# Turning the expert outputs by transposing transfers in place of TensorE turns, batches 0 to 6

## The chip, the cores and the metric

The kernel runs on one core of a Trainium2 chip. The time is device microseconds of one execution; lower is better. Three runs of the kernel before took 242.09 to 243.47 us, with a median of 242.59 us. A trace is one further execution, taken by the hardware profiler. Its engines are PE (TensorE: matmuls and turns; its weight loads are listed as PEld), ACT (ScalarE), DVE (VectorE), POOL (GpSimd) and SP (SyncE, which here only issues DMAs).

## What is computed

Two stages over 8 batches of 576 tokens. The first is attention with 8 heads of 64 and a window of 32 tokens to either side. Its output, 576x512 per batch, goes through four attention experts: each projects it to q, k and v of width 64, does causal attention, and projects back to 512 with its own `wo`. A gate picks two of the four experts for each token and weights them.

```
scores = scale * np.matmul(q, k.transpose(0, 1, 3, 2))        # window of 32
x = (softmax(scores) @ v).transpose(0, 2, 1, 3).reshape(B, S, 512)
logits = x @ w_gate                                           # top 2 of 4, softmax over them
for e in range(4):
    qe, ke, ve = x @ wq[e], x @ wk[e], x @ wv[e]
    a = causal_softmax(scale * (qe @ ke.transpose(0, 2, 1)))
    out += weight_of_e * (a @ ve @ wo[e])
```

## The kernel before

The whole program is one list of steps, `ORDER`, written out by hand. Each engine gets its instructions in the order in which the steps stand in the list, and works them off in that order; the framework adds the semaphores from what each step reads and writes. A step is a name with digits, then `@` with its banks of PSUM, and `:` with the engine that does it: `a` ACT, `v` DVE, `g` POOL. `ot31:v@0` is thus step `ot` for batch 3 and expert pair 1, on DVE, from bank 0. All eight banks are one tile `PS`, dealt out by the numbers in the list.

Loads (`lq`, `lk`, `lv`: q, k and v), the moves on chip that pair heads (`mv`, four DMAs each, L366) and the stores (`st`, L727 and L730) are all issued by SP. A load also waits until PE has reached the load's place in the list (`load`, L195 to L200), so that SP can't run ahead of it; `mv` and `st` wait only for their data. SP issues in the order of the list too: a DMA whose data isn't ready holds up those behind it.

For one batch the steps that matter here run as follows. The four experts are worked in two pairs `j`.

- `po` (L640, PE): attention weights times values, into two banks.
- `oe` (L649, DVE): divides by the row sums, multiplies by the gate, and writes `OE`, 128 tokens x (5 token tiles x 2 experts x 64) in bf16. There are two such buffers, one a pair.
- `pt` (L658, PE): turns `OE` by five matmuls against the identity, 128x128 each, into one bank.
- `ot` (L663, ACT or DVE): copies that bank into `OTT`, expert width on the partitions and tokens along the row. `OTT` has two buffers, one for even and one for odd batches, and a half in each for a pair.
- `py` (L703, PE): times `wo`, both pairs added in PSUM; three parts, of 256, 256 and 64 tokens.
- `ye` (L719, ACT or DVE) copies the result out of PSUM and `st` stores it.

Batch 7 is the last, and its second pair is worked in three parts (`pw`, `ow`, `tw`, `uw`), so that the end of the program overlaps better. Its first pair uses `po`, `oe`, `pt` and `ot`.

The helpers `mm` (L189) and `turn_pe` (L192) issue all matmuls and all turns, so the profile shows those at L190 and L193; copies by `copy` stand at L182 (ACT) and L184 (DVE, POOL). Several stages share L190: the names of the tiles tell them apart. `PS<-WO,OTT` is `py`, `PS<-ident_bf,OE` is `pt` (and `tw`), `PS<-T` is the window scores (`sc`), `PS<-WV,XTB` is `pv`.

Of the kernel before, what the change touches and what calls it, by code (L numbers as in the profile page):

```python
# [20 lines left out]
HS = 288  # L21
# [3 lines left out]
NOE = 2  # L25
# [24 lines left out]
    po01@2 pt00@0 oe01@2 ot00:a@0 vc20:g qc31:g pp111@4 kc31:g mv31 pe111:a@4 lv32 lv33 ps102@6 mk2100:g vc21:g  # L50
    pt01@0 se100 ps103@1 xe103@1 xe102@6 se102 tq400:e qc40:g ps110@4 xe110@4 se110 pv11@3 ve11:a@3 av23@1 av20@6
    ot01:v@0 un23@1 mk3011:g py02@5 ye02:a@5 av24@0 lq410:e ps113@1 xe113@1 lk410:e un20@6 tk400:e ps112@4 xe112@4
    un24@0 ps111@6 xe111@6 py01@2 av21@4 un21@4 av22@6 un22@6 ye01:a@2 se113 sc311@02 ex3111@2 sc310@46 tq410:e
    ex3110@0 kc40:g mv40 st02 mk3001:g ex3101@6 se112 ex3100@4 lk500:e mk3010:g xt20@2 xf20:a@2 xt21@0 xf21:a@0
    xt22@6 lv30 xf22:v@6 se101 se103 po10@4 oe10@4 py00@2 ye00:a@2 sc400@06 ex4000@0 st01 ex4001@6 lq500:e
    mk3101:g lv42 sc401@24 xb20:g ex4011@4 se111 po11@0 lv34 lk510:e qc41:g ex4010@2 pt10@7 xb22:v xb21:g tk410:e
    pp201@5 pe201:a@5 pp200@2 kc41:a lv41 ga2@6 pe200:a@2 ps200@2 tk500:e ps203@4 st00 xe203@4 mv41 oe11@0 ps202@0
    xe202@0 xe200@2 ot10:v@7 pt11@7 ot11:a@7 gt2 pp210@4 mk3100:v mk3000:g vc31:g pe210:v@4 tq500:e pp211@0
    mk3110:g mk3111:g av33@2 pv21@7 un33@2 vc30:g av31@4 un31@4 lq510:e mk4010:g qc50:g ve21:a@7 pe211:a@0 ge2
    lv43 av34@7 un34@7 py11@0 ye11:a@0 mk4001:g py10@2 ye10:a@2 py12@7 ye12:a@7 av30@4 gm2 gu2@6 av32@0 xt32@6  # L60
    un30@4 xf32:a@6 sc410@24 un32@0 kc50:g mv50 xb32:g lv52 mk4011:v ex4101@4 mk4101:g ex4100@2 mk4100:g sc411@06
    ex4110@0 tq510:e qc51:g mk4110:g lk600:e lv40 xt31@4 xf31:a@4 lq600:e se200 xb31:v xt30@2 xf30:a@2 pv20@0
    ve20:v@0 ps213@2 ex4111@6 mk4111:g lv44 vc41:g xe213@2 se213 xb30:v tk510:e vc40:g ps212@4 xe212@4 mk4000:g
    sc501@26 ex5010@2 ex5011@6 sc500@04 ex5000@0 lv53 mk5000:g tk600:e ex5001@4 pp300@2 pp301@0 pe300:a@2 kc51:a
    se203 ps201@4 xe201@4 tq600:e pe301:a@0 ps211@2 ga3@7 xe211@2 gt3 kc60:g mv51 gm3 pp311@5 pe311:a@5 ps210@0
    xe210@0 se210 lv51 ps302@2 xe302@2 se211 pv31@4 av42@5 un42@5 ge3 ve31:a@4 vc50:g av43@0 un43@0 av40@2 un40@2
    ps301@5 xe301@5 lk610:e se301 av44@4 un44@4 qc60:a pp310@0 pe310:a@0 gu3@7 xt41@4 xf41:v@4 mk5010:g ps300@2
    xe300@2 se202 av41@6 un41@6 ps303@0 sc511@24 xe303@0 mv60 se212 mk5001:v ex5110@2 ex5111@4 lq610:e sc510@06
    lv54 lv50 mk5110:g tk610:e kc61:v lq700:e ex5101@6 ex5100@0 xt40@2 xf40:a@2 xb41:g xb40:g pv30@4 ve30:a@4
    xt42@0 xf42:v@0 sc600@26 ex6001@6 xb42:g ex6000@2 lk710:e mk5101:v sc601@04 ex6011@4 ex6010@0 lk700:e pp400@6  # L70
    se201 po20@2 mk5011:g pe400:a@6 tq610:e qc61:g ps313@0 xe313@0 ps312@4 oe20@2 tq700:e ps311@6 xe311@6 pp411@0
    pt20@2 lq710:e xe312@4 ot20:a@2 pe411:a@0 mk5100:g po21@6 oe21@6 pp401@4 vc51:g ga4@3 mk5111:g pe401:a@4
    ps403@6 xe403@6 ps401@4 xe401@4 ps310@0 xe310@0 tk700:e kc70:g mk6001:g pv41@2 ve41:a@2 av51@6 un51@6 qc70:g
    gt4 ge4 av52@4 un52@4 av50@0 se310 pt21@2 ot21:a@2 se302 st11 un50@0 mv61 pv40@6 mv70 gm4 ve40:a@6 xt50@4
    gu4@3 mk6011:g ps402@0 av54@2 un54@2 lv60 xf50:a@4 xb50:g lv64 se401 av53@6 lv70 un53@6 xe402@0 sc610@24
    ex6100@2 lv62 ex6101@4 lv63 sc611@06 ps400@2 ex6111@6 xe400@2 tq710:e mk6101:g py21@4 pp410@6 pe410:v@6
    ex6110@0 ye21:a@4 lv61 st10 lv71 se402 xt51@2 xt52@0 xf52:v@0 xf51:a@2 se312 xb52:a mk6100:g sc701@46 ex7010@4
    sc700@02 ex7001@2 xb51:v pp500@4 ex7000@0 mk6000:g tk710:e lv73 pp501@2 st12 ex7011@6 se303 se313 se311 po31@6
    oe31@6 lv72 pe501:a@2 pp511@2 pe511:v@2 st21 mk6111:g se300 po30@0 oe30@0 pe500:a@4 qc71:a ps503@6 ps502@4
    xe503@6 mk6010:v xe502@4 ps411@2 xe411@2 vc60:g ga5@7 gt5 ps410@0 xe410@0 ps501@5 ge5 pt31@4 ot31:v@4 pp510@2  # L80
    pt30@4 pe510:v@2 mk6110:g kc71:g vc61:g py20@0 xe501@5 gm5 av61@2 av60@5 ot30:a@4 un61@2 ye20:a@0 gu5@7 un60@5
    av63@0 un63@0 av62@2 un62@2 py22@7 ye22:v@7 ps413@4 xe413@4 av64@6 mv71 sc711@04 un64@6 ex7110@0 xt60@2
    ex7111@4 se502 xt62@6 st22 lv74 xf62:v@6 xf60:a@2 xb60:v py31@0 mk7011:g sc710@46 ye31:a@0 st31 ex7101@6 se413
    mk7110:g ex7100@4 mk7100:v xt61@2 xf61:a@2 ps412@0 xe412@0 mk7111:g pv50@6 se501 st20 se403 se400 po40@2
    oe40@2 ga6@0 ve50:a@6 gt6 ps513@6 xe513@6 mk7001:g ps500@4 xb62:g ps510@2 xe500@4 pt40@1 xb61:g xe510@2 vc71:v
    pp601@6 pe601:a@6 mk7000:g pp600@4 pe600:a@4 ge6 se410 ot40:v@1 se411 se412 po41@2 pp611@4 pe611:a@4 py30@6
    mk7010:g se500 ye30:a@6 pv61@1 py32@4 ye32:a@4 ve61:a@1 oe41@2 gm6 gu6@0 vc70:g av72@2 un72@2 ps602@6 xe602@6
    ps600@4 av73@0 mk7101:g un73@0 av70@2 un70@2 xe600@4 ps603@6 ps601@4 xe603@6 pt41@0 ot41:v@0 xe601@4 pp610@6
    pe610:a@6 ps511@4 ps512@2 xe512@2 se601 se512 xe511@4 se510 st30 se503 av74@0 un74@0 av71@6 pv51@0 un71@6
    py42@1 ve51:a@0 st32 ye42:v@1 st42 xt72@2 xf72:a@2 xt71@4 xf71:a@4 xb72:g xt70@6 xf70:a@6 xb70:v xb71:v  # L90
    ps611@0 py41@2 py40@4 ye41:a@2 ye40:a@4 po50@6 xe611@0 pv60@2 ve60:a@2 pp700@0 se600 st41 oe50@6 ps610@6
    xe610@6 pe700:v@0 se602 ps612@2 xe612@2 se513 st40 se511 po51@4 pp710@0 oe51@4 pt50@2 pp711@6 se611 se612
    ot50:v@2 pe711:a@6 pt51@2 pe710:v@0 ot51:a@2 se603 po60@4 ps613@6 se610 xe613@6 se613 ps711@0 ps710@2 xe710@2
    se710 xe711@0 pp701@6 pe701:a@6 oe60@4 pt60@4 po61@2 oe61@2 py50@0 ye50:a@0 st50 ot60:a@4 py51@6 ye51:v@6
    ps702@2 py52@5 ye52:a@5 st51 pv71@0 ga7@1 ve71:v@0 gt7 xe702@2 se702 st52 ps701@6 ps703@2 xe703@2 ps700@4
    se703 xe701@6 se701 xe700@4 pt61@0 ot61:v@0 pv70@2 gm7 py60@6 ge7 ye60:a@6 ve70:v@2 py61@4 st60 ye61:a@4
    ps712@2 st61 xe712@2 se711 gu7@1 pw710@0 ow710@0 se700 po70@6 oe70@6 py62@4 ye62:a@4 st62 ps713@0 tw710@5
    se712 pt70@6 ot70:v@6 pw711@7 ow711@7 uw710:a@5 py70@4 tw711@7 uw711:v@7 xe713@0 se713 pw712@6 ye70:a@4 st70
    py71@0 ye71:a@0 st71 ow712@6 tw712@7 uw712:a@7 py72@7 ye72:v@7 st72
# [4 lines left out]
def kernel(  # L104
# [84 lines left out]
    def mm(*a, **kw):  # L189
        last_pe[0] = nc.tensor.matmul(*a, **kw)  # L190
# [363 lines left out]

    def pp(c, b, j, n, b0):
        W = XTB[b % 2]
        for half in range(2):
            for dt in range(NDT):
                mm(PS[:, b0 + half, 0:HS], WQK[j][n][:, dt, :], W[:, dt, HS * half:HS * half + HS],
                   start=(dt == 0), stop=(dt == NDT - 1))  # L560
# [5 lines left out]
    def pv(c, b, part, b0):  # L566
        W = XTB[b % 2]
        if part == 0:
            for t in range(4):
                for dt in range(NDT):  # L570
                    mm(PS[:, b0 + t // 2, 256 * (t % 2):256 * (t % 2) + 256], W[:, dt, 128 * t:128 * t + 128], WV[:, dt, :],
                       start=(dt == 0), stop=(dt == NDT - 1))
        else:
            for dt in range(NDT):
                for j in range(2):
                    mm(PS[64 * j:64 * j + 64, b0, 0:128], W[:, dt, 512:576], WV[:, dt, 128 * j:128 * j + 128],
                       start=(dt == 0), stop=(dt == NDT - 1), skip_group_check=True)
# [14 lines left out]
    def ps(c, b, j, ch, b0):  # L592
        Q = QKE[(2 * b + j) % len(QKE)]
        for kt, lo, hi, at in CHUNKS[ch]:
            for eo in range(2):
                r = slice(64 * eo, 64 * eo + 64)
                if ch < 3:
                    mm(PS[:, b0 + eo, at:at + hi - lo], Q[r, 1, 128 * kt:128 * kt + 128], Q[r, 0, lo:hi],
                       start=True, stop=True, skip_group_check=True)
                else:  # L600

                    mm(PS[:, b0 + eo, 0:64], Q[r, 1, 512 - 64 * j:640 - 64 * j], Q[r, 0, 512:576],
                       start=True, stop=True, skip_group_check=True)
# [61 lines left out]


# [107 lines left out]
```

## Time and profile before

| | |
|---|---|
| median of three runs | 242.59 us (242.09 to 243.47) |
| the profiled execution | 243.22 us; span of its instructions 240.3 us |
| granted TensorE clock | 0.997 |
| busy: PE, DVE, ACT, POOL | 213.4, 190.9, 164.8, 144.8 us |
| DMA packets of SP's queue | 56864, 46.94 MB, 70.5% of 16 engines' span |
| turns of `OE` by PE | 80 matmuls, 7.5 us |
| copies into `OTT`, ACT and DVE | 9 and 9 |

Times in the profile are us from the first instruction, durations in ns where they are so called. A group of instructions is given by line, engine, operation, the tiles out<-in, the shapes, then count, busy us and mean ns, and the idle time just before them with what ended it. "SPq" marks DMA instructions of SP. The span is divided among stages that overlap: while one batch is in the experts, the next ones are in the window attention and in loading.

### The profile page before, as it was taken

What the parts mean: (1) busy time and instruction counts of PE and PEld (TensorE: products, weight loads), DVE (VectorE), ACT (ScalarE), POOL (GpSimd) and SP (SyncE); (2) the same over time, 40 slices, a digit from 0 to 9 for tenths busy, and PEclk for the clock granted to TensorE, in tenths of its full rate; (3) what the DMA queues carried; (4) which work ended last, traced back from release to release, by engine and by line L of the source; (5) the groups of instructions that cost most, each with busy time, mean ns of one, the idle gap of its engine ahead of it and who ended that gap; (6) DMA issues with size and microseconds to landing.
All of it is one profiled execution on the core that took longest, in us unless ns stands there. A gap on an engine that the chain in (4) does not pass through costs nothing.

```text
span 240.3 us, 10580 instructions
## 1 busy us (share of the span) xinstructions
PE 213.4 (89%) x4537; PEld 166.5 (69%) x4548; DVE 190.9 (79%) x350; ACT 164.8 (69%) x260; POOL 144.8 (60%) x189
## 2 busy tenths in 40 slices
PE   7877789797998999789999999989899959999981
PEld 2656676676876778569777888867597738776650
DVE  4789998697797969998999899678876995554770
ACT  2665467886689577556895886686829748967761
POOL 7005162444897796955998997699709961621310
PEclk9999999999999999999999999999999999999998
DMA  6999898999799889987976887698605120130555
GB/s 211 303 268 296 195 292 213 283 303 240 243 257 267 228 237 290 285 244 169 274 157 185 226 286 255 154 208 222 194 5 176 45 100 14 58 144 3 199 196 196
DMA packets 57486, 48.79 MB, mean 203 GB/s; under 512 B 40544, under 2 KB 43104, under 8 KB 57440
## 3 DMA queue, kind: packets, MB, share of 16 engines
q1 hardware_dynamic: 56864, 46.94, 70.5%
q10 hardware_dynamic: 576, 1.18, 1.4%
q8 instruction: 35, 0.57, 1.0%
q14 instruction: 11, 0.09, 0.1%
HBM read 30.42 MB, written 9.44 MB: 166 GB/s over the span
## 4 chain that ended last, share of the span: by engine, by line
PE 57%; DVE 15%; POOL 7%; issue 7%; DMA 5%; ACT 4%; SPq 2%; ACTq 0%; DVEq 0%; POOLq 0%
PE PS L190 50%; PE PS L193 6%; POOL A L422 4%; DVE T L184 3%; DMA V<-in_v_dram 3%; DVE T L317 2%; DMA T<-T 2%; ACT XTF L182 2%; SPq L196 2%; ACT A L418 2%; PE PS L237 1%; POOL V L184 1%; DVE OE L655 1%; POOL ATE L619 1%; DVE XN L451 1%
## 5 line engine op out<-in xcount | busy, mean ns | idle before, releaser
L422 POOL TENSOR_TENSOR A<-A,MASKP 128x576 f32<-128x576 f32 x40 | 57.6, 1448 | 5.0 <-ACT A L418 4.8
L619 POOL TENSOR_SCALAR_AFFINE_SELECT ATE<-ATE 128x256 bf16<-128x256 bf16 (+1 forms) x80 | 32.0, 419 | 38.6 <-ACT ATE L614 30.7
L614 ACT ACTIVATE ATE<-PS 128x1024 bf16<-128x1024 f32 x48 | 47.5, 1029 | 6.4 <-PE PS L190 6.4
L418 ACT ACTIVATE A<-PS 128x576 f32<-128x576 f32 x64 | 38.2, 652 | 14.0 <-PE PS L190 13.4
L190 PE MATMUL PS<-V,A 128*64 128x65 f32 (+1 forms) x1280 | 39.7, 223 | 4.8 <-POOL V L184 1.8
L190 PEld LDWEIGHTS PS<-V,A 128*64 128x64 f32 (+1 forms) x1280 | 36.1, 132 | 9.3 <-issue 3.0
L190 PE MATMUL PS<-T 64*64 64x128 f32 (+3 forms) x1280 | 39.7, 263 | 1.2 <-ACT XTF L182 0.6
L190 PEld LDWEIGHTS PS<-T 64*64 64x64 f32 x1280 | 33.7, 133 | 4.5 <-issue 1.8
L184 POOL COPY V<-V 64x1536 f32<-64x1536 f32 (+1 forms) x14 | 24.1, 1723 | 18.7 <-DMA V<-in_v_dram 16.5
L317 DVE STREAM_TRANSPOSE T<-qn 128x1152 f32<-128x1152 f32 x14 | 32.6, 2329 | 3.2 <-PE PS L190 2.7
L317 DVE STREAM_TRANSPOSE T<-kn 128x1152 f32<-128x1152 f32 x14 | 32.3, 2330 | 0.8 <-PE PS L190 0.5
L182 ACT COPY XTF<-PS 128x1024 f32<-128x1024 f32 (+1 forms) x21 | 17.2, 832 | 10.1 <-PE PS L193 8.3
L184 POOL CAST XTB<-XTF 128x128 bf16<-128x128 f32 (+1 forms) x21 | 15.5, 758 | 13.3 <-ACT XTF L182 12.9
L182 ACT COPY Y<-PS 128x1024 f32<-128x1024 f32 (+1 forms) x20 | 16.8, 858 | 9.4 <-PE PS L190 6.4
L451 DVE TENSOR_TENSOR XN<-PS,RC 128x512 f32<-128x512 f32 x32 | 22.1, 691 | 1.3 <-DVE RC L450 0.2
L190 PE MATMUL PS<-WO,OTT 128*128 128x512 bf16 (+1 forms) x85 | 18.6, 341 | 2.4 <-ACT OTT L182 1.1
L190 PE MATMUL PS<-WV,XTB 128*128 128x256 bf16 (+1 forms) x192 | 18.5, 256 | 2.0 <-DVE OTT L184 1.9
L182 ACT CAST QKE<-PS 128x576 bf16<-128x576 f32 x25 | 15.9, 642 | 5.4 <-PE PS L190 5.2
L190 PE MATMUL PS<-QKE 64*128 64x64 bf16 (+4 forms) x192 | 17.5, 277 | 2.0 <-DVE OE L655 1.4
L190 PE MATMUL PS<-XTB,WK 128*128 128x288 bf16 x128 | 18.3, 286 | 0.0
L190 PE MATMUL PS<-XTB,WQ 128*128 128x288 bf16 x128 | 18.0, 286 | 0.0
L190 PEld LDWEIGHTS <-XTB 128*128 128x128 bf16 (+1 forms) x192 | 14.3, 102 | 5.0 <-issue 3.4
(88 smaller groups left out, 319.0 us busy)
## 6 DMA issues: line engine op xcount, KB each, us to landing
V<-in_v_dram SPq DMA_DIRECT2D x32, 256.0 KB, 5.3
out_dram<-Y SPq DMA_DIRECT2D x16, 512.0 KB, 3.3
kn<-in_k_dram SPq DMA_DIRECT2D x28, 288.0 KB, 4.9
qn<-in_q_dram SPq DMA_DIRECT2D x28, 288.0 KB, 4.8
T<-T SPq DMA_DIRECT2D x56, 144.0 KB, 3.8
V<-in_v_dram SPq DMA_DIRECT2D x8, 128.0 KB, 5.6
out_dram<-Y SPq DMA_DIRECT2D x16, 64.0 KB, 3.1
qn<-in_q_dram SPq DMA_DIRECT2D x2, 320.0 KB, 4.8
```

Of the source, the lines that this page charges most:

```text
L182: nc.scalar.copy(o, i)
L184: eng(c).tensor_copy(o, i)
L190: last_pe[0] = nc.tensor.matmul(*a, **kw)
L193: last_pe[0] = nc.tensor.transpose(*a)
L196: r = q_.dma_start(o, i)
L237: nc.tensor.matmul(one(a[-1]), WARM[:, 0:128], WARM, start=True, stop=True, skip_group_check=True)
L317: nc.vector.transpose(T.rearrange("q h (p o) -> q h o p", o=18)[:, :, o0:o1, :], x[:, :, o0:o1, :])
L418: nc.scalar.activation(AT[(2 * b + g) % NAT_][half][p], two(b0)[:, :, 0:HS], EXP, scale=scale_att)
L422: eng(c).tensor_tensor(out=ap, in0=ap, in1=MASK[:, None, HS * half:HS * half + HS].to_broadcast([128, 2, HS]), op=MULT)
L451: nc.vector.tensor_tensor(out=XN[T // 2][:, T % 2, :].rearrange("p (t h d) -> p h t d", t=4, h=8), in0=u[:, :, 0:64].rearrange("p h (d t) ...
L614: nc.scalar.activation(chunk(A, ch), two(b0), EXP, scale=scale_moe)
L619: nc.gpsimd.affine_select(ap, ap, pattern=[[0, n], [1, w]], compare_op=IS_GE, fill=0.0, base=0, channel_multiplier=-1)
```

## The change

For batches 0 to 6, each `pt` and its `ot` are replaced by one step `dt`: a transposing DMA from `OE` to `OTT`, issued by SP, 14 in all. It stands in the list where `pt` stood, and the `ot` is gone. Batch 7 stays as it was. All other steps, their order, their banks and engines are the same. The transfer writes all 640 columns of its half of `OTT`, the copy wrote 576; nothing reads the last 64.

```diff
+    def dt(c, b, j):
+
+        nc.sync.dma_start_transpose(OTT[b % 2][:, j, :].rearrange("p (t c) -> p t c", c=128),
+                                    OE[(2 * b + j) % NOE][:, :, :, :].rearrange("p t e d -> p (t e d)"))
...
-    po01@2 pt00@0 oe01@2 ot00:a@0 vc20:g qc31:g pp111@4 kc31:g mv31 pe111:a@4 lv32 lv33 ps102@6 mk2100:g vc21:g
-    pt01@0 se100 ps103@1 xe103@1 xe102@6 se102 tq400:e qc40:g ps110@4 xe110@4 se110 pv11@3 ve11:a@3 av23@1 av20@6
-    ot01:v@0 un23@1 mk3011:g py02@5 ye02:a@5 av24@0 lq410:e ps113@1 xe113@1 lk410:e un20@6 tk400:e ps112@4 xe112@4
+    po01@2 dt00 oe01@2 vc20:g qc31:g pp111@4 kc31:g mv31 pe111:a@4 lv32 lv33 ps102@6 mk2100:g vc21:g dt01 se100
+    ps103@1 xe103@1 xe102@6 se102 tq400:e qc40:g ps110@4 xe110@4 se110 pv11@3 ve11:a@3 av23@1 av20@6 un23@1
+    mk3011:g py02@5 ye02:a@5 av24@0 lq410:e ps113@1 xe113@1 lk410:e un20@6 tk400:e ps112@4 xe112@4 un24@0 ps111@6
...
-    se703 xe701@6 se701 xe700@4 pt61@0 ot61:v@0 pv70@2 gm7 py60@6 ge7 ye60:a@6 ve70:v@2 py61@4 st60 ye61:a@4
+    se703 xe701@6 se701 xe700@4 dt61 pv70@2 gm7 py60@6 ge7 ye60:a@6 ve70:v@2 py61@4 st60 ye61:a@4 ps712@2 st61
```

The DMAs on SP's queue around the new steps, in their order, are then: `lk400 dt00 mv31 lv32 lv33 dt01 lq410`; `lk510 dt10 lv41 st00 mv41 dt11 lq510`; `lk700 dt20 lq710 dt21 st11 mv61 mv70`; `st21 dt31 dt30 mv71`; `st20 dt40 dt41 st30`; `st40 dt50 dt51 dt60 st50 st51 st52 dt61 st60`.

The diff also gives the matmul steps `pp`, `pv`, `ps` and `py` a way to write only half of the partitions at a time, for steps marked `q`. No step of the list is marked so, and these matmuls are the same as before.

## The prediction

> **What bounds the kernel now.** The page first. Its share of the chain of work that ended last says who sets the end:
>
> ```profile
> PE 57%; DVE 15%; POOL 7%; issue 7%; DMA 5%; ACT 4%; SPq 2%; ACTq 0%; DVEq 0%; POOLq 0%
> ```
>
> TensorE (PE) is on the chain more than half the time, so taking work off PE can pay, but only where PE is what everything waits for. Hence the second view, the chain in order of time. Its columns are start in us, us, and what:
>
> ```profile
> 68.05 7.02 DMA V<-in_v_dram
> 75.19 1.90 POOL V L184
> 77.14 3.89 PE PS L190 x107
> 81.08 4.93 PE PS L190 x127
> ...
> 99.28 0.41 PE PS L193 x5
> ...
> 171.61 0.46 DVE OTT L184
> 172.11 0.44 PE PS L193 x5
> ...
> 224.33 0.39 PE PS L193 x5
> ```
>
> The reader is to see two things. Up to 77.14 the chain runs through a load of V, so the two turns of batch 0 (`pt00`, `pt01`, at 73 and 75 us) are not on it. The pieces "L193 x5" are the turns of the expert outputs that are on it: nine of them, the first and the last shown, 3.31 us together; and one copy out of PSUM, 0.46 us.
>
> **What goes.** The groups of instructions, with count, busy us and mean ns:
>
> ```profile
> L193 PE MATMUL PS<-ident_bf,OE 128*128 128x128 bf16 x80 | 7.5, 220 | 1.7 <-DVE OTT L184 0.9 <-DVE OE L655 0.8
> ...
> L182 ACT COPY OTT<-PS 128x576 bf16<-128x576 bf16 x7 | 4.5, 642 | 0.3 <-PE PS L193 0.3
> ...
> L184 DVE COPY OTT<-PS 128x576 bf16<-128x576 bf16 x8 | 3.6, 451 | 1.1 <-PE PS L193 1.1
> ```
>
> Seventy of the 80 turns go, 70/80 x 7.5 = 6.6 us of PE, with seven ACT copies (7 x 0.642 = 4.5 us) and seven DVE copies (7 x 0.451 = 3.2 us). The copies lie beside PE work except the one on the chain. So the gain is bounded by 0 and by 6.6 us of PE plus 0.46 us plus one more wait, which the PE timeline shows in brackets:
>
> ```profile
> 195.42 0.41 PE L190 MATMUL PS<-WV,XTB 128*64 128x128 bf16 x8 [1.85 <-DVE OTT L184]
> ```
>
> There `pv61` waits 1.85 us for the copy `ot40`; but PE then waits again, for POOL, so the chain passes it by. Upper bound 6.6 + 0.46 + 1.85 = 8.9 us. I take what the chain holds: 3.31 + 0.46 = **3.8 us gained**. What is late next there is PE itself, on the following step of the list.
>
> **What comes.** Fourteen transfers on SP's queue, each 128x640 bf16 = 160 KB, from `OE` to `OTT`. The trace has no transposing transfer, so its two costs are bounded by neighbours: how long SP is held, and how long from issue to landing. First the on-chip moves of `mv` (ns min/median/max of the issue, and us to landing), then from the page a load, `mv` again with its size, and a small store, then the landing of all loads of L196:
>
> ```profile
> L366 SPq DMA_DIRECT2D T<-T x56: 508/588/1592, 25.3 to 171.0; - x56
> ...
> DMA to landing us min/median/max: 2.4/3.8/5.6
> ```
>
> ```profile
> V<-in_v_dram SPq DMA_DIRECT2D x32, 256.0 KB, 5.3
> ...
> T<-T SPq DMA_DIRECT2D x56, 144.0 KB, 3.8
> ...
> out_dram<-Y SPq DMA_DIRECT2D x16, 64.0 KB, 3.1
> ```
>
> ```profile
> DMA to landing us min/median/max: 2.8/5.2/9.0
> ```
>
> Held: 0.51 to 1.59 us, I take `mv`'s median, 0.59. Landing: 2.4 to 9.0 us. By place and size `mv` is nearest (3.8); by piece it is the load of V, which moves rows of 64 f32 = 256 bytes, as the transfer moves 128 bf16 = 256 bytes of a token tile (5.3). I take **4.5 us**, between them, while loads run, and 3.1 (the small store's) in the last 30 us, where SP issues stores alone.
>
> The Trainium skill speaks against the change: "VectorE: DVE Perf Modes", section "The three transpose paths", gives 1309 ns for a 128x128 bf16 block by DMA and 390 by TensorE. Here a TensorE turn takes 220 ns, so the second figure isn't this kernel's; no run yet shows the first. Five blocks one after the other would make 6.5 us of landing, an estimate from that page, and the sum below would then come out near 260 us.
>
> **Where it falls on the path.** SP works its queue in order. A transfer waits there for its `oe`, and behind it wait the loads, moves and stores of the list; its reader is `py`, on PE, which is in order too. The distance from the turn to `py` was a matter of the list, which stays. Three places are too short.
>
> *Batch 0.* On SP the order is `dt00 mv31 lv32 lv33 dt01`. SP's timeline (`mv31`, then the two loads of V), the expert output that `dt01` needs, and the PE step that reads it (`py02`):
>
> ```profile
> 74.07 2.46 SPq L366 DMA_DIRECT2D T<-T  x4
> 76.64 2.68 SPq L196 DMA_DIRECT2D V<-in_v_dram  x2
> ```
>
> ```profile
> 73.85 0.82 DVE L655 TENSOR_TENSOR OE<-PS,RG 128x640 bf16<-128x640 f32 x1
> ```
>
> ```profile
> 78.94 0.27 PE L190 MATMUL PS<-WO,OTT 128*64 128x256 bf16 x1
> ```
>
> The output is there at 74.67, but SP is through `lv33` only at 76.64 + 2.68 = 79.32, plus 0.59 for `dt00` = 79.91. Landing at 79.91 + 4.5 = 84.4. `py02` wanted it at 78.94 (the V chain sets that time, the turns saved don't). PE stands **5.5 us**.
>
> *Batch 1.* `dt11` comes right behind `mv41`, in a stretch where SP issues back to back:
>
> ```profile
> 99.33 2.86 SPq L366 DMA_DIRECT2D T<-T  x4
> ```
>
> ```profile
> 104.43 1.04 PE L190 MATMUL PS<-WO,OTT 128*128 128x512 bf16 x3
> ```
>
> `mv41` ends at 102.19, `dt10` ahead of it adds 0.59, landing at 102.78 + 4.5 = 107.28. `py11` without the turn `pt11` comes at 104.43 - 0.41 = 104.02: **3.3 us**.
>
> *Batch 6.* `dt61` stands behind the stores of batch 5 (`st52` last), and `py60` follows one step of PE later:
>
> ```profile
> 223.45 1.98 SPq L730 DMA_DIRECT2D out_dram<-Y  x2
> ```
>
> ```profile
> 226.30 1.03 PE L190 MATMUL PS<-WO,OTT 128*128 128x512 bf16 x3
> ```
>
> Issue at 225.43, landing at 225.43 + 3.1 = 228.53; `py60` is due at 226.30 - 0.39 = 225.91: **2.6 us**.
>
> The other eleven I cost at nothing, since their `py` is far off. The tightest is `dt51` (its `oe51`, then `py50`):
>
> ```profile
> 213.92 0.82 DVE L655 TENSOR_TENSOR OE<-PS,RG 128x640 bf16<-128x640 f32 x1
> ```
>
> ```profile
> 219.76 1.67 PE L190 MATMUL PS<-WO,OTT 128*128 128x512 bf16 x6
> ```
>
> From 214.74 to 219.76 less three turns of 0.44 is 3.7 us: 3.1 fits, 4.5 would cost 0.8. A wait that is new on SP: `dt21` needs `oe21` and stands ahead of `st11` and `mv61`, whose reader is `sc610` on PE:
>
> ```profile
> 144.16 0.82 DVE L655 TENSOR_TENSOR OE<-PS,RG 128x640 bf16<-128x640 f32 x1
> ```
>
> ```profile
> 143.61 9.76 SPq L366 DMA_DIRECT2D T<-T  x8
> ```
>
> ```profile
> 153.64 1.11 PE L190 MATMUL PS<-T 64*64 64x64 f32 x36
> ```
>
> `mv61` (the first four) slips from 143.61 to 144.98 + 0.59 = 145.6; with 2.46 for its four issues and 3.8 to land that is 151.9, before 153.64. Without that cover each us over it is a us of PE.
>
> **The sum.** 5.5 + 3.3 + 2.6 = 11.4 us of standing, less 3.8 gained: +7.6. The profiled run took 243.22 us (span 240.3), so 250.8; it is 0.63 above the median of the three runs, 242.59, and on that scale I say **250.2 us**. I count each standing us in full because while PE stands the queues of ACT, DVE and POOL soon reach a step that needs it, and none of the three places has PE waiting right after.
>
> **The rivals.**
>
> *The transfer is heavy.* It holds SP 1.59 us and lands after 9.0, the longest of the rows above. Then batch 0 costs 79.32 + 1.59 + 9.0 - 78.94 = 11.0, batch 1 8.8, batch 6 8.5, and `dt51` 9.0 - 3.7 = 5.3: 33.6 - 3.8 = +29.8, 272.4 us. For it: 640 pieces of 256 bytes and a transposing path that no row shows. Against: on-chip moves land sooner than loads. The Trainium skill's page is on its side, part of the way.
>
> *Part is given back.* After each stop the engines find the rings emptier and PSUM banks free, and half of the 11.4 is regained: +1.9, 244.5 us. Against: the chain behind `py02` is PE without a break until 81.08 + 4.93 = 86 us.
>
> *Faster: the transfer lands as quickly as the quickest `mv`, and PE is worth its full busy time.* With 2.4 us the three places cost 3.4 + 1.2 + 1.9 = 6.5; the gain is the upper bound, 8.9: -2.4, 240.2 us. It decides from the point where the gain passes the standing: 6.5 us at 2.4 us of landing. For it: the 1.85 us wait of PE that goes too. Against: the chain holds 3.8 of the 8.9, and `dt01` can't start before SP is through `lv33`, however fast it is.
>
> **How the numbers follow.** Forecast 0.50; heavy 0.22; given back 0.14; faster 0.14. A measurement of this kernel tells some 0.5% (1.2 us) from no change. Faster by more than that: 0.13; within it: 0.08, where "given back" and "faster" meet; slower 0.79. The forecast's own bounds, landing 2.4 with 6.6 us gained to landing 5.6 with 3.8, give 242.4 to 256.9 us (18.1 us of standing, `dt51` among it); to hold 8 in 10 the range runs from 242 (most of the faster case left out) to 268 (the top of the heavy case left out).
>
> **What would show it.** PE should list waits for a DMA `OTT<-OE` at `py02`, `py11` and `py60`, of 5.5, 3.3 and 2.6 us, and none at `py21` or `py42`; the transfers 0.6 us each on SP and 3 to 5 to landing; turns of `OE` down to 10, PE busy down by 6.6 us. If the transfers hold SP for over 2 us, or land after 7, the heavy case is right and `mv61` and `py50` will wait too. If PE doesn't wait at `py02`, my reading of SP's order is wrong.

## The result and the profile after

| | before | after |
|---|---|---|
| median of four runs | 242.96 us (242.09 to 243.47) | 253.83 us (252.37 to 255.38) |
| the profiled execution: time, span | 243.22, 240.3 us | 252.37, 250.6 us |
| granted TensorE clock | 0.997 | 0.977 |
| busy: PE, DVE, ACT, POOL | 213.4, 190.9, 164.8, 144.8 us | 214.6, 185.5, 160.5, 143.9 us |

The changed kernel is slower: the ratio is 1.0471, with a 95% interval of 1.042 to 1.0522. (Here and below the ratios leave disturbed runs out, so one needn't be the quotient of the medians beside it.) The forecast was +7.6 us; the medians are 10.9 apart, the two profiled spans 10.3.

The page of the kernel after, the lines that answer to those of before: busy time, SP's DMA queue, the chain by engine, and the median landing of the on-chip moves `mv` (the last number).

```profile
PE 214.6 (86%) x4467; PEld 165.4 (66%) x4478; DVE 185.5 (74%) x343; ACT 160.5 (64%) x253; POOL 143.9 (57%) x189
...
q1 hardware_dynamic: 66272, 49.24, 79.0%
...
PE 50%; DMA 15%; DVE 15%; POOL 7%; issue 6%; ACT 3%; SPq 1%; ACTq 0%; DVEq 0%; POOLq 0%
...
T<-T SPq DMA_DIRECT2D x56, 144.0 KB, 4.5
```

DMA went from 5% of the chain to 15%. PE's busy time should have fallen by the 6.6 us of its turns and rose by 1.2. The queue carries (66272 - 56864) / 14 = 672 packets more for each transfer, and `mv` lands in 4.5 us where it took 3.8.

The groups of instructions of the kernel after. Ten turns of `OE` are left, and `py` now has idle time ahead of it, nearly all of it put down to the transfer:

```profile
L189 PE MATMUL PS<-WO,OTT 128*128 128x512 bf16 (+1 forms) x85 | 19.4, 354 | 12.1 <-DMA OTT<-OE 10.1 <-ACT OTT L181 1.1 <-issue 0.2
...
L192 PE MATMUL PS<-ident_bf,OE 128*128 128x128 bf16 x10 | 1.2, 222 | 0.8 <-DVE OE L658 0.8
```

Where those 10.1 us stand, in PE's timeline of the kernel after (the brackets hold the idle time ahead of a row): `py02`, `py11` and `py60`, the three places forecast and no others.

```profile
83.39 0.42 PE L189 MATMUL PS<-WO,OTT 128*64 128x256 bf16 x2 [5.23 <-DMA OTT<-OE]
...
114.64 1.46 PE L189 MATMUL PS<-WO,OTT 128*128 128x512 bf16 x6 [3.72 <-DMA OTT<-OE]
...
236.97 1.24 PE L189 MATMUL PS<-WO,OTT 128*128 128x512 bf16 x5 [1.20 <-DMA OTT<-OE]
```

The chain in order of time, kernel after, has each of the three transfers on it, from issue to landing:

```profile
78.32 5.03 DMA OTT<-OE
...
109.49 4.88 DMA OTT<-OE
...
234.08 2.62 DMA OTT<-OE
```

SP's own timeline says why each started so late. The output that `dt01` carries was there at 72.81 (`oe01`, on DVE), before the first of these rows began, yet `dt01` is the fourth:

```profile
72.96 1.32 SPq L671 DMA_TRANSPOSE OTT<-OE  x1
74.38 2.48 SPq L365 DMA_DIRECT2D T<-T  x4
76.96 1.26 SPq L195 DMA_DIRECT2D V<-in_v_dram  x2
78.32 2.90 SPq L671 DMA_TRANSPOSE OTT<-OE  x1
```

```profile
106.15 3.24 SPq L365 DMA_DIRECT2D T<-T  x4
109.49 1.26 SPq L671 DMA_TRANSPOSE OTT<-OE  x1
```

```profile
232.42 1.56 SPq L740 DMA_DIRECT2D out_dram<-Y  x2
234.08 1.25 SPq L671 DMA_TRANSPOSE OTT<-OE  x1
```

And the tile `OTT` of the kernel after: how long the fourteen hold SP (ns min/median/max), and their landing (us):

```profile
L671 SPq DMA_TRANSPOSE OTT<-OE x14: 1200/1253/2900, 73.0 to 234.1; - x14
...
DMA to landing us min/median/max: 2.6/4.4/5.4
```

The three stops make 10.15 us. But PE was also slower behind the first one. The stretches of the kernel after (columns: us; PE, PEld, DVE, ACT, POOL busy with counts; granted clock; DMA share; GB/s), one behind `py02` and one later:

```profile
83.40:88.80 5.40, 5.18 (x69) 3.07 (x72) 0.60 (x2) 3.60 (x5) 3.27 (x6) 0.50 0.52 158
204.90:208.20 3.30, 3.01 (x40) 2.23 (x42) 2.47 (x11) 0.34 (x1) 0.25 (x1) 0.50 0.47 128
```

The clock is 0.50 in both. The same steps, from `av24` to `sc311`, first in PE's timeline before, then after:

```profile
79.37 0.67 PE L190 MATMUL PS<-V,A 128*32 128x65 f32 x32
...
81.61 2.09 PE L190 MATMUL PS<-V,A 128*64 128x65 f32 x64
83.62 2.40 PE L190 MATMUL PS<-T 64*64 64x64 f32 x80
```

```profile
83.75 1.10 PE L189 MATMUL PS<-V,A 128*32 128x65 f32 x32
...
87.61 2.63 PE L189 MATMUL PS<-V,A 128*64 128x65 f32 x64
90.17 2.12 PE L189 MATMUL PS<-T 64*64 64x64 f32 x70
```

Before they take 83.62 - 79.37 = 4.25 us, after 90.17 - 83.75 = 6.42: **2.2 us** more for the same matmuls. This is a second price of the stop that the forecast did not have. The clock records of the trace have the half clock from 81.99 to 88.81, beginning while PE still stands.

### The profile page after: what moved, and what is told of

Same layout as the page of the kernel before. It is cut to its first block, busy times and chain, and to the rows that moved or that the text cites. A ratio compares the mean times of both kernels' runs of the same rounds, so it can differ in the third digit from the quotient of the medians.

```text
span 250.6 us, 10451 instructions
## 1 busy us (share of the span) xinstructions
PE 214.6 (86%) x4467; PEld 165.4 (66%) x4478; DVE 185.5 (74%) x343; ACT 160.5 (64%) x253; POOL 143.9 (57%) x189
## 3 DMA queue, kind: packets, MB, share of 16 engines
q1 hardware_dynamic: 66272, 49.24, 79.0%
## 4 chain that ended last, share of the span: by engine, by line
PE 50%; DMA 15%; DVE 15%; POOL 7%; issue 6%; ACT 3%; SPq 1%; ACTq 0%; DVEq 0%; POOLq 0%
PE PS L189 45%; DMA OTT<-OE 5%; DMA qn<-in_q_dram 5%; PE PS L192 4%; POOL A L421 4%; DVE T L316 3%; DVE T L183 3%; DMA V<-in_v_dram 3%; DMA kn<-in_k_dram 3%; DVE XN L450 2%; PE PS L236 1%; POOL V L183 1%; POOL ATE L622 1%; DVE OE L658 1%; ACT XTF L181 1%
## 5 line engine op out<-in xcount | busy, mean ns | idle before, releaser
L622 POOL TENSOR_SCALAR_AFFINE_SELECT ATE<-ATE 128x256 bf16<-128x256 bf16 (+1 forms) x80 | 31.0, 406 | 45.0 <-ACT ATE L617 32.7
L189 PE MATMUL PS<-V,A 128*64 128x65 f32 (+1 forms) x1280 | 41.1, 229 | 5.1 <-POOL A L421 2.2
L189 PEld LDWEIGHTS PS<-V,A 128*64 128x64 f32 (+1 forms) x1280 | 37.7, 137 | 10.1 <-POOL A L421 2.5
L189 PE MATMUL PS<-T 64*64 64x128 f32 (+3 forms) x1280 | 40.8, 263 | 2.6 <-DMA T<-T 0.8
L189 PEld LDWEIGHTS PS<-T 64*64 64x64 f32 x1280 | 34.3, 133 | 6.4 <-issue 2.6
L189 PE MATMUL PS<-WO,OTT 128*128 128x512 bf16 (+1 forms) x85 | 19.4, 354 | 12.1 <-DMA OTT<-OE 10.1
L189 PE MATMUL PS<-QKE 64*128 64x64 bf16 (+4 forms) x192 | 18.2, 289 | 2.2 <-DVE OE L658 1.3
L189 PEld LDWEIGHTS <-OTT 128*128 128x128 bf16 (+1 forms) x96 | 7.1, 103 | 18.7 <-DMA OTT<-OE 10.6
```

The source lines that it names most:

```text
L622: nc.gpsimd.affine_select(ap, ap, pattern=[[0, n], [1, w]], compare_op=IS_GE, fill=0.0, base=0, channel_multiplier=-1)
```

## The experiments

Three theories. **A**: the loss is the three stops, and the half clock follows from the first of them. **B**: the loss comes from the load that the transfers put on the DMA rings, and stays wherever they stand. **C**: the stops count, but the half clock doesn't hang on the stop. Line numbers in these kernels differ by some lines from those of the kernel after.

### dt01 moved forward on SP's queue

The kernel after, with one step moved:

```diff
-    po01@2 dt00 oe01@2 vc20:g qc31:g pp111@4 kc31:g mv31 pe111:a@4 lv32 lv33 ps102@6 mk2100:g vc21:g dt01 se100
+    po01@2 dt00 oe01@2 dt01 vc20:g qc31:g pp111@4 kc31:g mv31 pe111:a@4 lv32 lv33 ps102@6 mk2100:g vc21:g se100
```

> The kernel after with one step moved: dt01 stands right behind oe01, so on SP's queue it is ahead of mv31, lv32 and lv33. Theory A (queue place): the 5.2 us that PE stands before py02 go, and with them most of the 6.8 us of half clock behind it (some 2 us of PE time): 253.8 falls to about 246.5, and PE shows no wait for OTT at py02. Rival B (the transfers themselves weigh on SP and on the rings, 1.25 us of SP each): the wait only moves to mv31 and the loads of V behind it: 251 us or more. Rival C (the half clock is no consequence of the wait): falls by the wait alone, to about 248.6.

Measured: 247.12 us (246.11 to 250.25, four runs), ratio to before 1.0111 (1.0008 to 1.0215). SP's timeline has `dt00` and `dt01` together, ahead of `mv31`; PE's has `py02` with no wait in front of it:

```profile
72.76 2.63 SPq L669 DMA_TRANSPOSE OTT<-OE  x2
75.48 2.49 SPq L363 DMA_DIRECT2D T<-T  x4
```

```profile
77.56 0.27 PE L187 MATMUL PS<-WO,OTT 128*64 128x256 bf16 x1
```

The transfer is the same one; only its place in the queue changed, and some 6.7 us of median came back, more than the 5.2 of the stop itself. That fits A, whose price for stop and half clock is 7.4, and goes against B. C's 248.6 lies within the spread of the four runs, so the time doesn't rule C out. The stop at `py11` is longer in this trace, 4.52 us in place of 3.72, and now it has half clock behind it, from 107.54 to 110.96; `py02` has none.

### All three moved forward

```diff
-    mk2100:g vc21:g dt01 se100
...
-    ps203@4 st00 xe203@4 mv41 oe11@0 ps202@0 xe202@0 xe200@2 dt11 gt2
...
-    se703 xe701@6 se701 xe700@4 dt61 pv70@2
+    po01@2 dt00 oe01@2 dt01 vc20:g
...
+    ps203@4 st00 xe203@4 oe11@0 dt11 mv41 ps202@0 xe202@0 xe200@2 gt2
...
+    po61@2 oe61@2 dt61 py50@0
```

> The kernel after with three transfers earlier on SP's queue: dt01 right behind oe01, dt11 right behind oe11 and ahead of mv41, dt61 right behind oe61 and ahead of the stores of batch 5. Theory A: all three waits go (5.2 + 3.7 + 1.2 us, and some 2 us of half clock): 253.8 falls to about 241.5, slightly below the 243.0 of before. Rival B: 249 or more. Rival C: about 243.7.

Measured: 248.49 us (244.3 to 250.57, five runs), ratio 1.0229 (1.0122 to 1.0337). By the median this is B's number, 249; the quickest of the five runs, 244.3, is near C's 243.7, and it is the profiled one. The interval overlaps that of moving `dt01` alone, so the time doesn't tell the two kernels apart. PE's waits in it:

```profile
PE PS L186 <- DMA T<-T: 3.0, 4, 1.5
...
PE PS L186 <- DMA OTT<-OE: 1.8, 1, 1.8
```

Two stops are gone and the third is 1.8 us: `dt11`, now issued at 101.97, took 6.3 us to land. PE now waits for `mv` as well, 3.0 us where the kernel before has 0.2. The longest of these waits, 1.5 us at 91.36, is for `mv40`; it comes before `dt11` is issued, so moving `dt11` ahead of `mv41` isn't its reason. The trace also has two stretches of half clock, at 92.7 and 198.5. Two of the three stops went as A says, but A's 241.5 was too good: other losses, 1 to 3 us each, came in another place, and what brings them isn't told apart here.

### The three turned by TensorE, eleven by transfer

Batches 0 (second pair), 1 (second) and 6 (second) keep `pt` and `ot`; the rest is as in the kernel after.

```diff
-    mk2100:g vc21:g dt01 se100
...
-    xe202@0 xe200@2 dt11 gt2
...
-    xe701@6 se701 xe700@4 dt61 pv70@2
+    mk2100:g vc21:g pt01@0 se100
...
+    av23@1 av20@6 ot01:v@0 un23@1
...
+    xe202@0 xe200@2 pt11@7 ot11:a@7 gt2
...
+    xe701@6 se701 xe700@4 pt61@0 ot61:v@0 pv70@2
```

> Eleven pairs by transfer, and the three whose transfer comes too late (01, 11, 61) by TensorE turn and copy as before. Theory A: nothing waits, and the eleven turns that are off PE gain some 3 us: about 240.5 against 243.0. Rival B (the transfers weigh on SP and the rings wherever they stand): 246 or more, in proportion eleven fourteenths of the loss.

Measured: 244.8 us, four runs from 240.78 to 247.52, too far apart for an interval. No PE wait for a transfer is left in the profile, as A has it; but the profiled run, at 247.52 the slowest of the four, has half clock in four places (at 31.9, 79.7, 117.3 and 202.6). The lowest run is A's number, the median is near B's. By time this is inconclusive.

### The wait at py02 filled

The kernel after, with 18 matmuls that compute nothing used, 512 columns each, in front of `py02`:

```diff
-    mk3011:g py02@5
+    mk3011:g fl9@5 fl9@5 py02@5
...
+    def fl(c, n, b0):
+        for _ in range(n):
+            nc.tensor.matmul(one(b0), WO[:, 0, 0:128], WO[:, 0, :], start=True, stop=True, skip_group_check=True)
```

> The kernel after with 18 matmuls of 512 columns, whose result nobody reads, on PE just ahead of py02, so that PE works for about 4 of the 5.2 us that it stands there. The wait itself stays. Theory A with the clock as its consequence: no half clock behind py02, and 253.8 falls by about 2 to 251.7. Rival C (what is slow behind the wait is not the clock's doing): unchanged, 253.8, within 0.7.

Measured: 252.68 us (250.16 to 254.72, four runs), ratio 1.027 (1.0138 to 1.0401). The median lies between the two numbers. The ratio's interval lies below that of the kernel after, 1.042 to 1.0522, which is A's side, but the runs are 4.6 us apart, so the time alone doesn't decide between A and C. The trace does, by the stretch and by the same steps as above in PE's timeline:

```profile
84.50:88.70 4.20, 4.20 (x116) 3.13 (x116) 1.39 (x4) 3.44 (x5) 2.91 (x5) 1.00 0.57 182
```

```profile
79.82 4.39 PE L675 MATMUL PS<-WO 128*128 128x512 bf16 x18
...
84.48 0.67 PE L187 MATMUL PS<-V,A 128*32 128x65 f32 x32
...
88.64 1.62 PE L187 MATMUL PS<-T 64*64 64x64 f32 x51
```

With PE kept busy while it waits, the clock behind the stop is 1.00, and the steps take 88.64 - 84.48 = 4.16 us, as before, in place of 6.42. So the idle PE is what brought the half clock there, and it cost 2.2 us. Two other traces agree: with `dt01` moved forward there is neither stop nor half clock at this place, and with only the three late transfers (below) PE stands 5.27 us and has half clock from 83.74 to 87.15. The filled kernel isn't free of it, though: its trace has one stretch of half clock ahead of the filled place, from 77.11 to 80.52, behind a wait of 1.67 us for POOL. The step there took 3.31 us in place of 2.02, at a time when PE would have had to stand anyway.

The Trainium skill, "TensorE: Matmul & The Clock Gate", Part 1, says that the clock falls to half after an idle window of about 3.4 us, and that these windows run by themselves, not from the kernel's start. The two stretches of half clock in the kernel after last 6.83 and 3.41 us, two windows and one, so at this place the trace agrees. Counted back from 81.99, one whole step of 3.41 us (78.58 to 81.99) lies within the stop at `py02`. The stop of 3.72 us at `py11` is cut by such a step into 1.79 and 1.94 us, and the clock behind it stayed at 1.00. Waits of 2.25 us with half clock behind them, further below, are shorter than the page's window; there the measurement differs.

### Transfers added to the kernel before

The kernel before, all turns kept, plus eight transfers (batches 0, 1, 2 and 5) at the places of `dt`. They write the half of `OTT` that the other parity uses, and nobody waits to read them.

```diff
+    def dx(c, b, j):
+        nc.sync.dma_start_transpose(OTT[(b + 1) % 2][:, j, :].rearrange("p (t c) -> p t c", c=128),
+                                    OE[(2 * b + j) % NOE][:, :, :, :].rearrange("p t e d -> p (t e d)"))
...
-    mk2100:g vc21:g pt01@0 se100
+    mk2100:g vc21:g dx01 pt01@0 se100
```

> The kernel before, all turns and copies kept, with eight transposing transfers added at their places (both pairs of batches 0, 1, 2 and 5); each writes the OTT buffer of the other parity, which the next batch overwrites before it is read, so no step reads what they bring. They cost SP 1.25 us each and the rings about 2, and no wait of PE. Theory A (the loss is the wait of py for a late transfer, and the clock behind it): 243 to 245. Rival B (the transfers slow the loads and moves by their load on SP and the rings): eight fourteenths of the 10.9 us lost plus the 3.8 gained, 251.

Measured: 245.95 us (243.69 to 248.81, four runs), ratio 1.0116 (1.0019 to 1.0214). So the transfers alone, with no reader, seem to cost a little: 1.2%, some 2.8 us of 242, with an interval that begins just above nothing. That is far from B's 251 and near A's 243 to 245. The profile, of a run of 247.78 us, the second slowest of the four, lists these waits of PE:

```profile
PE PS L188 <- DMA T<-T: 6.7, 11, 1.8
```

These are eleven waits for `mv`, 6.7 us, where the kernel before has one of 0.2. `mv` stands behind the transfers on SP and shares the DMA rings with them, but that this is the reason is not shown: the first two of the eleven, 1.84 us at 68.20 and 0.43 us at 69.25, come before the first transfer is issued, at 75.15, and the quicker runs have no trace.

### Only the three late ones by transfer

```diff
-    mk2100:g vc21:g pt01@0 se100
...
-    av23@1 av20@6 ot01:v@0 un23@1
...
-    xe200@2 ot10:v@7 pt11@7 ot11:a@7 gt2
...
-    se701 xe700@4 pt61@0 ot61:v@0 pv70@2
+    mk2100:g vc21:g dt01 se100
...
+    xe200@2 ot10:v@7 dt11 gt2
...
+    se701 xe700@4 dt61 pv70@2
```

> The complement of the kernel with three pairs on PE: only 01, 11 and 61 are turned by transfer, at the places where the change put them; the other eleven by TensorE. Theory A: the whole loss is here, 10.1 us of standing and some 2 of half clock, less three turns: 253 to 255. Rival B (loss in proportion to the number of transfers): 245.5.

Measured: 255.53 us (253.41 to 257.81, four runs), ratio 1.063 (1.0529 to 1.0731). The three make the whole loss by themselves. PE stands at the same three places as in the kernel after, for 5.27, 1.48 and 2.27 us:

```profile
PE PS L188 <- DMA OTT<-OE: 9.0, 3, 5.3
```

The interval lies just above that of the kernel after, 1.042 to 1.0522: the other eleven transfers, with the turns that they save, add nothing to the loss. This is A, against B's 245.5.

### Only transfers whose reader is far off

Eight pairs of batches 2 to 6 by transfer (20, 21, 30, 31, 41, 50, 51, 60), then also 40; the rest by TensorE as before. An extract:

```diff
-    xe311@6 pp411@0 pt20@2 lq710:e xe312@4 ot20:a@2 pe411:a@0
+    xe311@6 pp411@0 dt20 lq710:e xe312@4 pe411:a@0
...
-    pp701@6 pe701:a@6 oe60@4 pt60@4 po61@2 oe61@2 py50@0 ye50:a@0 st50 ot60:a@4 py51@6
+    pp701@6 pe701:a@6 oe60@4 dt60 po61@2 oe61@2 py50@0 ye50:a@0 st50 py51@6
```

> Only the eight pairs whose transfer has time and whose turn lay on the chain: 20, 21, 30, 31, 41, 50, 51, 60; batches 0 and 1 and the pairs 40 and 61 by TensorE. Theory A: no wait for OTT on PE, gains of 0.4 (batch 2), 1.2 (batch 3), 0.4 (41), 1.1 (batch 5), 0.3 (60): 3 us, 240 against 243. Rival B: 8/14 of the transfers' load, 247 or more.

> The late eight and pair 40 as well. In the traces so far, without the copy ot40 PE does two steps 1.9 us earlier and then stands 2.25 us in one piece for POOL, where it stood 1.85 and 0.61 in two; in each of these five traces the granted clock falls to a half just there for 3.4 us, and the step py42 comes 1.1 us later by the comparison with the steps before. Theory A: about 1 us above the kernel with eight, the half clock at 200 us in its trace and not in the other's. Rival (pair 40 is worth its turn, the half clock there is chance): 0.3 to 0.5 us below it.

Measured: 241.86 us with the eight (239.37 to 244.17, twelve runs), ratio 1.0016 (0.9973 to 1.0059), and 241.23 with 40 as well (238.65 to 245.85, twelve runs), ratio 0.9959 (0.991 to 1.0008). PE waits for no transfer in either, so A holds for the waits and B, at 247 or more, is out. A's 240 isn't reached: 40 of the 80 turns are gone, half of 7.5 us, and the time stays.

For the second kernel I had expected the half clock near 200, which the kernel after has at 204.9 behind a wait of 2.25 us. PE's timeline of the kernel with 40, and the stretch:

```profile
195.12 1.15 PE L187 MATMUL PS<-V,A 128*64 128x65 f32 x32 [2.25 <-POOL A L419]
```

```profile
195.10:198.50 3.40, 3.38 (x96) 2.98 (x98) 2.52 (x12) 1.78 (x2) 0.00 (x0) 1.00 0.82 44
```

The same wait is there, and the clock stays at 1.00. That theory falls. Of the seven traces that show this wait of 2.25 us, five have half clock behind it and two have not. Where it came, it cost 1.3 to 1.5 us: from the end of the wait to `py42` is 7.67 us in the kernel with 40, 8.98 in the kernel after and 9.15 to 9.18 in the other four. The 1.1 of the expectation was too small.

What looks like chance may be the place of the wait on the clock's steps. In the kernel after the two stretches begin 122.88 us apart, 36 times 3.413. Counted on such steps in each trace, the wait here is cut into 1.86 and 0.39 us, and that of the kernel with ten pairs (below), which has no half clock either, into 1.49 and 0.76; in the five traces with half clock at least 1.92 us lie in one step. The margin is thin and no run tests it.

### Ten late pairs, and the same with the wait filled

Batches 2 to 6 by transfer, `dt61` right behind its `oe61`, batches 0, 1 and 7 by TensorE; the second kernel adds eight matmuls that compute nothing used ahead of `av72`, where the 2.25 us were.

```diff
-    po61@2 oe61@2 py50@0
...
-    se701 xe700@4 pt61@0 ot61:v@0 pv70@2
+    po61@2 oe61@2 dt61 py50@0
...
+    se701 xe700@4 pv70@2
...
-    gu6@0 vc70:g av72@2
+    gu6@0 vc70:g fl8@5 av72@2
```

(the last pair of lines in the filled kernel only)

> The same without the filling. Theory A: 239.5 to 241, by whether the clock falls at 200 us in a run (1.1 us in the traces where it did). Rival: no difference to the filled one.

> The ten pairs of batches 2 to 6 by transfer, dt61 right behind oe61, batches 0 and 1 by TensorE; and 8 matmuls of 512 columns that nobody reads on PE ahead of av72, in the 2.25 us that PE stands there for POOL (a step of 1.7 us in it). Theory A: no wait for OTT, ten turns gained (2.4 us in the trace with nine, 0.4 more for 61), and no half clock at 195 to 205 us in any run: 239 against 242, and a narrower spread than without the filling. Rival (the filling only takes PE's time, the half clock comes where it likes): the same as without it, or 0.5 above.

Measured: 240.89 us unfilled (239.15 to 242.05, six runs), ratio 0.9933 (0.989 to 0.9977), and 240.75 filled (239.81 to 242.95, six runs), ratio 0.9949 (0.9904 to 0.9993). Both beat the kernel before by a little, less than 1%, and with it the kernel after. The filling makes no difference that can be measured, and the narrower spread expected of it didn't come (3.1 us with it, 2.9 without). Neither trace has half clock near 200 us, so the two don't test whether the filling keeps it away. In the unfilled kernel the wait for a transfer at `py60` is gone too; the one wait of `py` that its list of PE's waits still has is for a copy of batch 7:

```profile
PE PS L187 <- ACT OTT L179: 1.1, 1, 1.1
```

## Why the forecast came out as it did, step by step

The direction and the three places were right; the size was 3.3 us short (10.9 against 7.6, by the medians).

- **`py02`, forecast 5.5, measured 5.23.** SP reached `dt01` behind `mv31`, `lv32`, `lv33`, as the prediction read the order. Three sizes were off and nearly cancelled, which is luck: issue at 78.32, not 79.91 (`lv32` and `lv33` took 1.26 us to issue, not 2.68), landing 5.03, not 4.5, and PE there at 78.16, not 78.94. Moving `dt01` alone took the wait away, so the order in the queue is shown to be its cause.
- **`py11`, forecast 3.3, measured 3.72.** `dt11` was issued 0.1 us behind `mv41`'s end, and landed in 4.88 us.
- **`py60`, forecast 2.6, measured 1.20.** The landing was 2.62 us in place of 3.1, and SP got to `dt61` 1.69 us ahead of the moment when PE wanted it (236.97 - 1.20 - 234.08), not 0.48 ahead as computed. Against the times that the prediction used, `py60` is due 9.86 us later (235.77 for 225.91) and SP reaches `dt61` only 8.65 later (234.08 for 225.43), so the earlier stops probably gave this place some slack.
- **The other eleven at nothing: right for the waits.** No other `py` waits for a transfer, `py21` and `py42` among them. (In the range, the standing at a landing of 5.6 us adds up to 17.95, not 18.1; nothing hangs on it.)
- **SP held 0.59 us: wrong, 1.25.** The `mv` median was the wrong neighbour. It cost little here, because only one such holding stands ahead of each late transfer, and in batch 0 the loads behind it were issued faster.
- **Landing 4.5 and 3.1: right in size.** The median of all fourteen is 4.4. Four took 2.6, all in the last fifth or so, where the DMA share (as `--windows` gives it, packets' times added up) was 0.32 to 0.68 while they were under way; the other ten took 4.1 to 5.4. The estimate of 6.5 us that the prediction worked out from the Trainium skill ("VectorE: DVE Perf Modes", "The three transpose paths") is above the longest landing of this kernel, 5.4, and far above 2.6: five blocks in one transfer are not five times the page's 1309 ns. (In the runs above single transfers took longer, up to 7.0 us where they were added to the kernel before.) The heavy case fell with it: nothing landed after 7 us, `py50` has no wait, and PE's waits for `mv` stay at 0.8 us in all. Two transfers, `dt01` and `dt50`, did hold SP for 2.90 and 2.28 us, over the 2 that the prediction named as a sign of that case.
- **The step that failed: "I count each standing us in full".** A stop cost more than its length. Behind the stop at `py02` the clock was at half and the same steps took 2.2 us longer; filling the wait shows that this was the idle PE's doing. A second stretch of half clock at 204.9 took 1.3 us, by the comparison of steps given with the late pairs; the runs show that this one doesn't come each time. The sum lacked 2.2 to 3.5 us there. That this is just the size of the miss is partly luck: the stops came to 10.15 us where the sum had 11.4, and the time regained (see the gain, below) is 0.5 short of the 3.8.
- **PE's busy time, forecast down by 6.6 us, rose by 1.2.** The half clock makes the same matmuls busy for longer, some 3.5 us by the two comparisons; the rest isn't accounted for.
- **The gain of 3.8 us: only argued, and probably net.** Spans: 10.15 of stops and 3.5 of half clock make 13.65, the span grew by 10.3, so 3.3 us came back. That would be the turns' gain less what the transfers cost the rings. The second is likely more than nothing (+1.2% for eight transfers added to the kernel before), but neither is measured by itself in this kernel.
- **The rival "part is given back" and "faster"** gave +1.9 and -2.4 us. Measured is +10.9: the time regained, 3.3 us, is no more than the turns' gain that was forecast, and none of the stops was shorter than SP's order and the landing make it.

**What stays open.** Where the expected gain of the eight late transfers went, and why the three turned by TensorE gave no clear number. The load on the rings may take some of it; the runs of one kernel with transfers in the loaded stretch lie 3 to 7 us apart, and the half clock comes in pieces of 3.41 us where a short wait may or may not bring it. Which of these it was in each case isn't told apart by these runs.

## What to carry to other kernels

A transfer that replaces work of an engine begins when the queue that issues it gets to it: write down what stands ahead of it there, add the landing, and compare that with the moment its reader wants it, before counting what the engine saves. Turn over only what has time to spare: here ten of the fourteen, in the late batches and with `dt61` moved forward, made the kernel 0.7% faster (0.9933, 0.989 to 0.9977), all fourteen made it 4.7% slower. And a stop of PE of 4.5 to 5.3 us cost its length and then some in each of the three traces looked at here that have one, because the steps behind it ran at half clock; one of 3.72 us had none behind it.

## What the hardware showed that was not expected

- A transposing transfer of 160 KB holds SP for 1.20 to 2.90 us, 1.25 in the median, against 0.59 for one of the `mv` DMAs of 144 KB. Four of the fourteen landed in 2.6 us, at a DMA share of 0.32 to 0.68, and nine in 4.1 to 5.4 at a share above 1.0. One, `dt60`, took 4.2 at a share of 0.22, which isn't explained.
- It costs about 2.0 us of all 16 DMA engines: SP's queue rose from 70.5% of 240.3 us to 79.0% of 250.6, 28.6 us for the fourteen. That is 160 KB in 2.0 us, some 80 GB/s. What other packets lost by the company is in this number: the same division gives 1.4 us with the three moved forward (78.1% of 242.6) and 2.7 with eight added (77.6% of 245.9). The Trainium skill, "Advanced Engine Details and Errata", section "X-Bar Transpose (TRN2)", expects 350 to 400 GB/s and the speed of regular DMAs; the measurement differs, at least for pieces of 256 bytes.
- The half clock came in stretches of 3.41 us or twice that: after stops of 4.52, 5.23 and 5.27 us in three traces, after waits of 2.25 us in five traces of seven, and now and then after shorter ones (1.67 us in the filled kernel). After the stop of 3.72 us the clock stayed at 1.00.
